# Keys by head in 64x32 tiles, z and W as full products, and the last units of a fused attention and expert kernel ahead of their outputs

## The chip, the cores and the metric

The kernel runs on one core of a Trainium2 chip. The metric is the device time of one execution in microseconds. Its engines are named as in the profile: PE multiplies matrices, PEld loads PE's weights, DVE, ACT and POOL work element by element, SP only issues transfers. The transfers of a queue are issued in the order of its instructions.

## The reference

Two stages follow one another. The first is an attention without softmax: each query and key is multiplied by two small matrices S1 and S2, and the outer product of the two results is its feature vector of 64. The second is a gated feed-forward layer on the heads put side by side.

```python
batch, n_heads, seq, head_dim = (4, 4, 1088, 32)   # r = 8

def phi(x):
    a = np.einsum('rd,bhsd->bhsr', S1, x)
    b = np.einsum('rd,bhsd->bhsr', S2, x)
    return np.einsum('bhsi,bhsj->bhsij', a, b).reshape(*x.shape[:-1], r * r)
q_p, k_p = (phi(q), phi(k))
kv = np.einsum('bhsf,bhsd->bhfd', k_p, v)
z = np.sum(k_p, axis=2)
num = np.einsum('bhsf,bhfd->bhsd', q_p, kv)
den = np.einsum('bhsf,bhf->bhs', q_p, z)[..., None] + 1e-06
x = (num / den).transpose(0, 2, 1, 3).reshape(4352, 128)

gate = np.maximum(x @ w_gate, 0.0)                 # 128 -> 1536
val = x @ w_val
out = gate * val @ w_out                           # 1536 -> 128, float32
```

## The kernel before, in words

**The attention, one batch at a time.** A batch's keys lie on 128 partitions as two heads by 64 tokens, two pairs of heads beside each other (`load_pairs`), 17 tokens on each partition. DVE transposes them in blocks of 32 (`ke_t1`), PE multiplies them by S1 and S2 (`ke_ab`, L448) in float32, in four tiles of the array of 64 rows by 64 columns (a "64x64 tile"), first for one pair of heads and then for the other, both added up in the same two PSUM banks. DVE transposes the result back to tokens on partitions (`ke_t2`, L460, tile `abk`). POOL (for batch 0 partly DVE, from a copy in PSUM) forms the outer products `kp` (L329), PE multiplies them with v (`ke_kv`, L552), DVE masks the result into `kv_bd`. For the denominator PE multiplies `abk` with a part of itself (`ke_z`, L507: nine float32 products in 128x64 tiles, the even ones on one column tile and the odd ones on the other), DVE masks it (`zd`, L519), PE multiplies it by S1 (`ke_w`, L524: two products in 128x64 tiles), and DVE writes that as a further column of the weights `wst` with which the queries are multiplied (`ke_wst`, L532). So numerator and denominator of the queries of a batch wait for its z and W.

The queries come in groups: batch 0 in four pieces (1, 1, 2 and 4 token columns), batches 1 to 3 in one group each, and a last group with the remaining ninth column of all four batches. For each group DVE transposes q (`qt`), PE multiplies by `wst` (L653, the last group L658), DVE transposes back (`abq`, L668), DVE or POOL form `bw`, `dn`, `rd`, `an` and the outer products `qp`, these are transposed (by PE and ACT for batch 0 and the last group, L712 and L753; by a transfer on SP for the others, L742) into `pt`, PE multiplies with `kv_bd` (L719, L725: "num"), and ACT writes `xT` (L761).

**The feed-forward, in 102 units.** A unit is one bank of 512 values: one to four gate products (g) and as many value products (L791), a relu on ACT into `g_sb` (L802), a product on DVE into `ht` (L811), and four output products (L822, "out") that add into bank 7 (`OB`). After the 6 to 24 units of a part ACT evicts the bank (`e_evict`, L839) and SP stores it; the last group's store is four transfers, two on SP and two on ACT (L850), one for each batch.

**What sets the order.** All this is written down as tasks with estimated durations, a due time and a number of banks, and a small planner (`Plan`) puts them in an order by start times that it reckons itself; each engine then runs its instructions strictly in that order. Units are due every 830 ns from 12.5 us on; attention tasks become due backwards from the units that need them. The eight banks are shared: the attention may hold 3 once units run (`a_max`), units hold at most 5 (`f_max`), and 7 of the 8 are given out. In the gaps before the first unit PE runs products of zeros (L871) to keep its clock up.

**Loads.** k and q of batch 0 are loaded first by SP, v of batch 0 by POOL with a cast to float16 on the way (L261, L262), then POOL issues six loads of gate and value weights and later one of the output weights. The other batches' k, q and v are loaded by SP behind a small transfer that waits for the first weights; their v is cast by ACT (L546), each batch with its own buffer. ACT and, for batch 0, DVE zero the padding of some tiles (`fills`).

Of the kernel before, what the change touches and what calls it, by code (L numbers as in the profile page):

```python
# [9 lines left out]
FP32 = mybir.dt.float32  # L10
# [28 lines left out]
class Plan:  # L39
# [46 lines left out]
    def run(self, first_f):  # L86
# [13 lines left out]
        def find(t, now):  # L100

            held = sum(1 for o in owner if o == t.kind)
            most = self.f_max if t.kind == "f" else self.a_max if started_f else self.n_banks
# [26 lines left out]
        total = len(self.tasks)  # L130
        while len(out) < total:
# [48 lines left out]
            if t.kind == "f":  # L180
                started_f = True
            clock[t.eng] = est + t.occ
# [11 lines left out]
def kernel(  # L194
# [20 lines left out]
    T = 64  # L215
    C = S // T
    CA = (C + 1) // 2
    CB = C - CA
    NG = 10
    NH = 14  # L220
    Q0 = 4
# [15 lines left out]
    k_sb = [const.tile([128, 2, C * D], FP32, name=f"k_sb{b}") for b in range(B)]  # L237
    q_sb = [const.tile([128, 2, (C + 1) * D], FP32, name=f"q_sb{b}") for b in range(B)]
    v_sb = [const.tile([128, H, CA * D], FP16, name=f"v_sb{b}") for b in range(B)]
    v32 = [const.tile([128, H, CA * D], FP32, name=f"v32_{b}") if b else None for b in range(B)]  # L240
# [4 lines left out]
    def load_pairs(eng, dst, src, b, hp=None):  # L245
        x = src[b].rearrange("(x y) (t c) d -> (y t) x (c d)", y=2, c=C)
        if hp is None:
            eng.dma_start(out=dst[:, :, 0:C * D], in_=x)
        else:
            eng.dma_start(out=dst[:, hp, 0:C * D], in_=x[:, hp])  # L250
# [8 lines left out]
    def load_v(eng, dst, b):  # L259
        x = v[b].rearrange("h (t c) d -> t h (c d)", c=C)  # L260
        eng.dma_start(out=dst[0:T], in_=x[:, :, 0:CA * D])  # L261
        eng.dma_start(out=dst[T:128, :, 0:CB * D], in_=x[:, :, CA * D:])  # L262
# [3 lines left out]
    load_pairs(nc.sync, k_sb[0], k, 0, 0)  # L266
    load_pairs(nc.sync, k_sb[0], k, 0, 1)
    load_q0(nc.sync, 0)
    load_q0(nc.sync, 1)
# [4 lines left out]
    nc.scalar.activation(out=scr, in_=zero[0:1, 0:1], func=ACTF.Relu)  # L274

# [4 lines left out]
    maskz = const.tile([128, H, R], FP32, name="maskz")  # L280
    mz2 = const.tile([128, 2, H, R], FP32, name="mz2")
    nc.gpsimd.memset(mz2, 1.0)
    nc.gpsimd.affine_select(out=mz2, in_=mz2, compare_op=ALU.is_ge, fill=0.0, base=0,
                            pattern=[[-64, 2], [-2 * R, H], [0, R]], channel_multiplier=1)
    nc.gpsimd.affine_select(out=mz2, in_=mz2, compare_op=ALU.is_ge, fill=0.0, base=R - 1,
                            pattern=[[64, 2], [2 * R, H], [0, R]], channel_multiplier=-1)
# [6 lines left out]
    sk = const.tile([128, 2 * 5 * 2 * R], FP32, name="sk")  # L293
    s1r = const.tile([128, 2, D], FP32, name="s1r")
    wst = [const.tile([128, 2, 2, 32], FP32, name=f"wst{b}") for b in range(B)]
    kt = [const.tile([128, 2, C + 1, 32], FP32, name=f"kt{b}") for b in range(B)]
    abk = [const.tile([128, CA, 2, 32], FP32, name=f"abk{b}") for b in range(B)]
    kp = [const.tile([128, 2, CA, 128], FP16, name=f"kp{b}") for b in range(B)]
    zd = [const.tile([128, H * R], FP32, name=f"zd{b}") for b in range(B)]
# [3 lines left out]
    nc.vector.memset(sk, 0.0)  # L303
# [8 lines left out]
    nc.vector.tensor_tensor(out=maskz, in0=mz2[:, 0], in1=mz2[:, 1], op=ALU.add)  # L312

    def fills(b):
        for x in (wst[b], (v32[b] if b else v_sb[b])[T:128, :, CB * D:], kt[b][:, :, C], kv_bd[b]):
            if b == 0:
                nc.vector.memset(x, 0.0)
            else:
                shape = list(x.shape)
                z = zero[128 - shape[0]:128, 0:1]  # L320
                for _ in shape[2:]:
                    z = z.unsqueeze(1)
                nc.scalar.copy(out=x, in_=z.to_broadcast(shape))
# [22 lines left out]
    def pool(n):  # L346
# [3 lines left out]
    land = dict(k00=4100.0, k01=4800.0, q0=6600.0, q0b=8700.0, v0=8900.0, w0=10100.0, w1=11600.0,  # L350
                w2=13500.0, k1=15800.0, wo=17500.0, q1=21000.0, v1=24500.0, k2=25500.0, q2=27000.0)
# [5 lines left out]
    def e_s1(t):  # L357
        nc.tensor.matmul(ps[:, t.bank, 0:2 * D], sel.rearrange("r x f -> r (x f)"),
                         s16[:, 0:2].rearrange("f p d -> f (p d)"), start=True, stop=True)
# [3 lines left out]
    t_s1c = P.add("s1c", "ACT", **act(64), deps=[t_s1], frees=[t_s1],  # L363
                  emit=lambda t: nc.scalar.copy(out=s1r.rearrange("p a d -> p (a d)"),
                                                in_=ps[:, t_s1.bank, 0:2 * D]))
# [5 lines left out]
    def e_sk(t):  # L371
        for a in range(2):
            masked(sk.rearrange("p (x y) -> p x y", x=2)[:, :, 32 * a:32 * a + 2 * R], a)
# [9 lines left out]
    def prep(b):  # L383
        f = P.add(f"fill{b}", "ACT", 1100, 1170, emit=lambda t: fills(b), after=[t_w0[0]])
# [9 lines left out]
    l_v0 = P.add("ld_v0", "POOL", 1350, 1350, emit=lambda t: load_v(nc.gpsimd, v_sb[0], 0))  # L394
    prev = l_v0
# [6 lines left out]
    l_v0.due = 2000.0  # L402
# [7 lines left out]
    def e_later(t):  # L410
        nc.sync.dma_start(out=gate[:, 0, 0:8], in_=wg[0:1, 0:1, 0:16].bitcast(FP32))
        load_pairs(nc.sync, k_sb[1], k, 1)
        nc.sync.dma_start(out=gate[:, 1], in_=k_sb[1][0:1, 0:1, 0:16])
        load_pairs(nc.sync, q_sb[1], q, 1)
        load_v(nc.sync, v32[1], 1)
        load_pairs(nc.sync, k_sb[2], k, 2)
        load_pairs(nc.sync, q_sb[2], q, 2)
# [3 lines left out]
    for n, e in (("v2", lambda t: load_v(nc.sync, v32[2], 2)),  # L421
                 ("k3", lambda t: load_pairs(nc.sync, k_sb[3], k, 3)),
# [483 lines left out]
```

## Time and profile before

| what | us |
|---|---|
| median of 3 runs (lowest, highest) | 108.33 (108.26, 111.96) |
| the profiled execution, its own time | 108.27 |
| its span, first to last instruction | 106.6 |
| first gate product on PE | 13.03 |
| last gate or value product on PE starts | 99.70 |
| last output product starts | 101.26 |
| last eviction by ACT | 101.69 to 102.07 |
| 102 products of DVE for the units, mean of one | 0.673 |
| 102 relus of ACT, mean of one | 0.605 |

Spans of the profile are in microseconds, means of one instruction often in nanoseconds. A busy PE does not mean that it is at its peak. A group of instructions is named by its line, engine and operation, with out<-in by the program's names. "x18" counts instructions: a float32 product is two on PE, one for each pass over the columns. In the timeline and the chain of waits the first number is the start and the second the length of a merged stretch; in brackets stands how long the engine had been idle before and what ended that.

### The profile page before, as it was taken

To read this page: it belongs to the slowest core of one execution; us is meant where nothing else is said; L and a number is where in the kernel's file an instruction comes from. 1 tells how busy PE (TensorE), PEld (TensorE's weight loads), DVE (VectorE), ACT (ScalarE), POOL (GpSimd) and SP (SyncE) were. 2 spreads that over 40 slices of the span, in tenths; PEclk is the share of its full clock that TensorE was granted. 3 is DMA by queue.
4 is the path that set the end of the run, shared out by engine and by line. 5 is a ranking of instruction groups with operands and counts; after the bars stand their busy time and mean duration, and the time that the engine had idled before them with its cause. 6 is when DMAs were issued, how large, how long until landed. Compare 5 with 4: busy or idle time off the path is not lost.

```text
span 106.6 us, 3081 instructions
## 1 busy us (share of the span) xinstructions
PE 98.5 (92%) x1166; PEld 65.9 (62%) x1166; DVE 91.6 (86%) x199; ACT 78.8 (74%) x158; POOL 47.1 (44%) x69
## 2 busy tenths in 40 slices
PE   6998999999999999999999999999699999999810
PEld 6767788776565655655566656667365666569500
DVE  4669979999998998999999999999668988988900
ACT  4468289569982875999948859997689869899510
POOL 6999260899396950129729402296000004000000
PEclk9999999999999999999999999999999999999985
DMA  1999998992015899910580040004812100400400
GB/s 31 303 207 198 225 220 230 242 360 71 3 49 106 97 222 341 337 40 3 132 163 6 0 102 0 0 0 102 168 32 58 43 6 0 98 0 6 98 26 26
DMA packets 15999, 11.60 MB, mean 109 GB/s; under 512 B 8816, under 2 KB 13296, under 8 KB 15984
## 3 DMA queue, kind: packets, MB, share of 16 engines
q1 hardware_dynamic: 12824, 9.87, 36.7%
q0 software_dynamic: 2960, 1.46, 10.3%
q8 instruction: 9, 0.15, 0.6%
q10 hardware_dynamic: 200, 0.07, 0.3%
q14 instruction: 6, 0.05, 0.1%
HBM read 9.05 MB, written 2.23 MB: 106 GB/s over the span
## 4 chain that ended last, share of the span: by engine, by line
PE 72%; DVE 7%; DMA 7%; POOL 4%; issue 4%; DVEq 1%; SPq 0%; ACT 0%; POOLq 0%
PE ps L791 37%; PE ps L822 18%; PE ps L448 5%; DMA pt<-qp 4%; PE ps L653 3%; PE ps L719 3%; DMA k_sb<-in_k_dram 3%; POOL qp L329 3%; PE ps L507 2%; DVE abq L668 1%; PE ps L712 1%; DVE kp L329 1%; PE ps L552 1%; DVEq L901 1%; DVE qp L329 1%
## 5 line engine op out<-in xcount | busy, mean ns | idle before, releaser
L811 DVE TENSOR_TENSOR ht<-g_sb,ps 128x512 f16<-128x512 f16 x102 | 64.7, 673 | 4.9 <-ACT g_sb L802 2.2
L802 ACT ACTIVATE g_sb<-ps 128x512 f16<-128x512 f32 x102 | 58.6, 605 | 12.0 <-PE ps L791 10.1
L822 PEld LDWEIGHTS <-ht 128*128 128x128 f16 x408 | 29.7, 98 | 19.0 <-DVE ht L811 3.2
L822 PE MATMUL ps<-wo,ht 128*128 128x128 f16 x408 | 38.7, 219 | 0.4 <-DVE ht L811 0.4
L791 PE MATMUL ps<-xT,wv 128*128 128x512 f16 (+2 forms) x132 | 37.2, 331 | 0.0
L791 PE MATMUL ps<-xT,wg 128*128 128x512 f16 (+2 forms) x132 | 36.5, 331 | 0.0
L329 POOL TENSOR_TENSOR kp<-abk 128x640 f16<-128x640 f32 (+1 forms) x14 | 16.3, 1200 | 3.5 <-DVE abk L460 3.5
L329 POOL TENSOR_TENSOR qp<-an,abq 128x512 f16<-128x512 f32 x16 | 16.7, 1070 | 0.5
L678 POOL TENSOR_TENSOR bw<-abq 128x128 f32<-128x128 f32 (+1 forms) x9 | 3.8, 421 | 27.6 <-DVE abq L668 26.8
L791 PEld LDWEIGHTS <-wv 128*128 128x128 f16 x132 | 11.6, 98 | 3.2 <-issue 1.4
L791 PEld LDWEIGHTS <-wg 128*128 128x128 f16 x132 | 11.7, 98 | 1.9
L871 PE MATMUL ps<-zero 128*128 128x128 f16 x75 | 7.0, 254 | 1.1 <-DVE zero L272 1.1
L695 POOL TENSOR_TENSOR an<-abq,rd 128x256 f32<-128x256 f32 (+2 forms) x6 | 2.9, 480 | 11.2 <-DVE rd L692 11.2
L839 ACT ACTIVATE o_sb<-ps 128x512 f32<-128x512 f32 (+2 forms) x11 | 5.6, 505 | 2.4 <-PE ps L822 2.1
L668 DVE STREAM_TRANSPOSE abq<-ps 128x512 f32<-128x512 f32 (+2 forms) x11 | 6.4, 588 | 0.8 <-PE ps L653 0.7
L761 ACT CAST xT<-ps 128x512 f16<-128x512 f32 (+2 forms) x11 | 5.4, 493 | 2.1 <-PE ps L719 2.0
L438 DVE STREAM_TRANSPOSE kt<-k_sb 128x544 f32<-128x544 f32 x8 | 5.7, 731 | 0.9 <-DMA k_sb<-in_k_dram 0.9
L871 PEld LDWEIGHTS <-zero 128*128 128x128 f16 x75 | 5.6, 116 | 1.2 <-DVE zero L272 1.1
L719 PE MATMUL ps<-pt,kv_bd 128*128 128x512 f16 (+2 forms) x20 | 5.1, 337 | 1.1 <-DMA pt<-qp 1.1
L448 PE MATMUL ps<-kt,sk 64*64 64x288 f32 x64 | 5.4, 424 | 0.3 <-DVE kt L438 0.3
L753 ACT COPY pt<-ps 128x256 f16<-128x256 f16 (+2 forms) x5 | 2.9, 583 | 3.1 <-DVE abq L668 1.7
L653 PE MATMUL ps<-qt,wst 64*64 64x256 f32 (+3 forms) x112 | 4.9, 302 | 0.0
(75 smaller groups left out, 68.4 us busy)
## 6 DMA issues: line engine op xcount, KB each, us to landing
out_dram<-o_sb SPq DMA_DIRECT2D x14, 128.0 KB, 2.4
k_sb<-in_k_dram SPq DMA_DIRECT2D x3, 544.0 KB, 5.4
q_sb<-in_q_dram SPq DMA_DIRECT2D x3, 544.0 KB, 5.8
v<-in_v_dram SPq DMA_DIRECT2D x3, 288.0 KB, 5.0
v<-in_v_dram SPq DMA_DIRECT2D x3, 256.0 KB, 5.2
k_sb<-in_k_dram SPq DMA_DIRECT2D x2, 272.0 KB, 3.0
q_sb<-in_q_dram SPq DMA_DIRECT2D x3, 128.0 KB, 3.0
wg<-in_moe_w_gate_dram POOLq DMA_DIRECT2D x3, 128.0 KB, 5.3
```

Of the source, the lines that this page charges most:

```text
L329: eng.tensor_tensor(out=dst.rearrange("s x (i j) -> s x i j", i=R), in0=a[:, :, :, None].to_broadcast([128, n, R, R]), in1=b[:, :, None, : ...
L438: nc.vector.transpose(kt[b][:, hp, 0:C].rearrange("p c t -> p (c t)"), k_sb[b][:, hp])
L448: nc.tensor.matmul(ps[64 * st:64 * st + 64, first.bank + h2, 0:CA * 32], sk[r, 64 * hp:64 * hp + 64], kt[b][r, hp, CA * st:CA * st + CA].r ...
L653: nc.tensor.matmul(o, wst[G.bs[0]][r, hp].rearrange("p a f -> p (a f)"), G.qt[r, hp, st], start=True, stop=True, skip_group_check=True)
L668: nc.vector.transpose(G.ab[:, lo:hi].rearrange("p x h f -> p h x f"), ps[:, f.bank:f.bank + 2, lo * 32:hi * 32].rearrange("p h (x t) -> p ...
L719: nc.tensor.matmul(o, kv_bd[G.bs[0]][:, 2 * hp:2 * hp + 2].rearrange("f a d -> f (a d)"), G.ptc[:, hp, c0:c0 + n], start=hp == 0, stop=hp ...
L791: nc.tensor.matmul(ps[:, t.bank, y * W:(y + 1) * W], w[:, j], xT[:, p.col:p.col + W], start=True, stop=True)
L802: nc.scalar.activation(out=U.g_sb, in_=ps[:, g.bank], func=ACTF.Relu)
L811: nc.vector.tensor_tensor(out=U.ht, in0=U.g_sb, in1=ps[:, vv.bank], op=ALU.mult)
L822: nc.tensor.matmul(ps[:, OB, s * DM:(s + 1) * DM], U.ht[:, y * n * 128 + s * 128:y * n * 128 + (s + 1) * 128], wo[:, j], start=(j == 0 and ...
L839: nc.scalar.mul(out=o_sb[:, 0:n], in_=ps[:, OB, 0:n * DM].rearrange("p (s m) -> p s m", s=n), mul=1.0 / (XSCALE * XSCALE))
L871: nc.tensor.matmul(ps[:, OB, 0:128], zero, zero, start=True, stop=True)
```

## The change

Keys and their values lie differently: 128 partitions are four heads by 32 tokens (34 tokens on each), so that one transfer brings whole rows. The projection of keys uses 64x32 tiles: eight tiles (two pairs of heads by four groups of tokens), each with 9 x 32 columns, written once instead of added up over two. z takes two chunks of `abk` at a time as one full 128x128 product with 64 columns (five instead of nine, the tenth chunk is zeros), W two full products added up, and `wst` is written in two DVE instructions for the two halves of the partitions. Batch 0's v is loaded in float32 by four transfers, two on SP between the two parts of q and two on ACT, and cast by ACT; v of later batches comes by four transfers instead of two, and batches share two buffers. The k feature products are cut along tokens instead of head pairs. In the planner units hold up to 7 banks once no attention task is left, and gate, value, relu and product of unit u above 90 are due (u - 90) x 400 ns earlier, their outs not. The last group has an output bank of its own, is evicted in two halves by ACT and DVE and stored by two transfers of two batches each. Landing times and durations in the planner are changed too.

```diff
-            most = self.f_max if t.kind == "f" else self.a_max if started_f else self.n_banks
+            most = (self.f_max if n_att else self.n_banks) if t.kind == "f" else self.a_max if started_f else self.n_banks
...
-    load_pairs(nc.sync, k_sb[0], k, 0, 0)
-    load_pairs(nc.sync, k_sb[0], k, 0, 1)
+    load_k(nc.sync, 0, 0)
+    load_k(nc.sync, 0, 1)
     load_q0(nc.sync, 0)
+    load_v(nc.sync, 0, 0, 2)
     load_q0(nc.sync, 1)
...
     nc.scalar.activation(out=scr, in_=zero[0:1, 0:1], func=ACTF.Relu)
+    load_v(nc.scalar, 0, 2, 4)
...
-    l_v0 = P.add("ld_v0", "POOL", 1350, 1350, emit=lambda t: load_v(nc.gpsimd, v_sb[0], 0))
...
+    def load_v(eng, b, lo=0, hi=4):
+        x = v[b].rearrange("h (t c) d -> t h (c d)", c=KC)
+        for g in range(lo, hi):
+            n = min(CA, KC - CA * g) * D
+            eng.dma_start(out=v32[b % 2][32 * g:32 * g + 32, :, 0:n],
+                          in_=x[:, :, CA * g * D:CA * g * D + n])
...
+        def ke_ab(t, b, lo, hi, first):
+            for g in range(lo, hi):
+                for hp in range(2):
+                    r = slice(64 * hp, 64 * hp + 64)
                     nc.tensor.matmul(
-                        ps[64 * st:64 * st + 64, first.bank + h2, 0:CA * 32],
-                        sk[r, 64 * hp:64 * hp + 64],
-                        kt[b][r, hp, CA * st:CA * st + CA].rearrange("p c t -> p (c t)"),
-                        start=hp == 0, stop=hp == 1, skip_group_check=True)
+                        ps[32 * g:32 * g + 32, first.bank + hp, 0:CA * 32],
+                        sk[r].rearrange("p h f -> p (h f)"),
+                        kt[b][r, CA * g:CA * g + CA].rearrange("p c t -> p (c t)"),
+                        start=True, stop=True, skip_group_check=True)
...
         def ke_z(t, b, lo, hi, m):
-            for c in range(lo, hi):
-                x = c % 2
-                ab = abk[b][:, c].rearrange("p h f -> p (h f)")
-                nc.tensor.matmul(ps[64 * x:64 * x + 64, m.bank, 0:H * R], ab,
-                                 ab.rearrange("p (h f) -> p h f", h=H)[:, :, R:2 * R],
-                                 start=c < 2, stop=c >= CA - 2, skip_group_check=True)
+            for y in range(lo, hi):
+                nc.tensor.matmul(ps[:, m.bank, 0:2 * H * R],
+                                 abk[b][:, 2 * y:2 * y + 2].rearrange("p c x f -> p (c x f)"),
+                                 abk[b].rearrange("p c x (h f) -> p (c x h) f", h=2)[
+                                     :, 8 * y:8 * y + 8, R:2 * R],
+                                 start=y == 0, stop=y == CA // 2, skip_group_check=True)
...
         def ke_w(t, b, z):
+            for x in range(2):
+                nc.tensor.matmul(ps[:, z.bank, 64:64 + H * R],
+                                 s1r.rearrange("p a d -> p (a d)"),
+                                 zd[b][:, x * H * R:(x + 1) * H * R],
+                                 start=x == 0, stop=x == 1, skip_group_check=True)
...
         def ke_wst(t, b, z):
             for h2 in range(2):
+                r = slice(64 * h2, 64 * h2 + 64)
+                nc.vector.tensor_tensor(
+                    out=wst[b][r, :, :, 2 * R:3 * R],
...
+            ahead = max(0, u - AHEAD) * 400.0
+            g.due, vv.due = due - ahead, due - ahead + 220
...
-            o = P.add(f"out{u}", "PE", 230, 230 + 170, kind="f",
-                      deps=[mult, last_evict if i == 0 else None, ],
+            o = P.add(f"out{u}", "PE", 230, 230 + 170, kind="f", banks=1 if final and not own else 0,
+                      deps=[mult, last_evict if i == 0 and not final else None],
...
+        def e_last(t, G, x):
+            o_sb = f_o.tile([128, 4, DM], FP32, name="o_sb")
+            src = ps[:, own[0].bank, x * DM:(x + 1) * DM]
+            if x == 0:
+                nc.scalar.mul(out=o_sb[:, 0], in_=src, mul=1.0 / (XSCALE * XSCALE))
             else:
+                nc.vector.tensor_single_scalar(o_sb[:, 0], src, 1.0 / (XSCALE * XSCALE), op=ALU.mult)
+            dst = out[2 * x * S:2 * (x + 1) * S].rearrange("(t c) m -> t c m", c=C)
+            (nc.sync, nc.scalar)[x].dma_start(out=dst[:, G.c0], in_=o_sb[:, 0])
```

## The prediction

> **What bounds the kernel now.** I read the busy shares first, then the stretches, then the chain of waits in order of time, and last the timeline of the start and of the end.
>
> ```profile
> PE 98.5 (92%) x1166; PEld 65.9 (62%) x1166; DVE 91.6 (86%) x199; ACT 78.8 (74%) x158; POOL 47.1 (44%) x69
> ```
>
> PE is the busiest engine, DVE is not far behind. Stretches (from:to, length, then busy time of PE, PEld, DVE, ACT, POOL, the granted clock, DMA share, GB/s):
>
> ```profile
> 20.00:40.00 20.00, 20.00 (x239) 12.99 (x238) 19.33 (x39) 14.78 (x27) 16.27 (x17) 1.00 0.58 138
> ...
> 76.00:77.10 1.10, 0.04 (x2) 0.02 (x2) 0.50 (x1) 0.44 (x1) 0.00 (x0) 1.00 0.97 183
> 77.10:90.00 12.90, 12.90 (x138) 7.98 (x139) 10.86 (x19) 10.77 (x20) 0.83 (x3) 1.00 0.15 32
> 90.00:102.00 12.00, 11.26 (x125) 8.04 (x122) 10.07 (x16) 9.99 (x20) 0.85 (x1) 1.00 0.19 45
> ```
>
> From 13 to 76 us PE has no gap at a clock of 1.00, so each 0.1 us of PE work taken out there is 0.1 us of the end, as long as DVE (idle 0.67 us in 20 to 40) keeps up. PE stands still only at 76 to 77 and after 99.
>
> ```profile
> 36.61 0.70 PE ps L507 x18
> 39.38 0.23 PE ps L524 x4
> 51.78 0.65 PE ps L448 x8
> 53.94 0.65 PE ps L448 x8
> 72.35 4.69 DMA pt<-qp
> ```
>
> These are pieces of the chain of waits (start, length): z (L507), W (L524) and k's projection (L448), batch by batch. Batch 1's projection stands there in one piece of 1.13 us.
>
> ```profile
> 6.27 0.29 PEld L358 LDWEIGHTS ps<-s,sel 16*128 16x128 f32 x2 [0.44 <-issue]
> 6.27 0.43 PE L358 MATMUL ps<-s,sel 16*128 16x64 f32 x2
> 7.07 0.66 PEld L507 LDWEIGHTS ps<-abk 128*64 128x64 f32 x18
> 7.89 0.18 DVE L519 TENSOR_TENSOR zd<-ps,maskz 128x32 f32<-128x32 f32 x1
> 8.59 0.18 DVE L532 TENSOR_TENSOR wst<-ps,maskw 128x32 f32<-128x32 f32 x1
> ...
> 101.26 0.40 PE L822 MATMUL ps<-wo,ht 128*128 128x128 f16 x4 [0.20 <-DVE ht L811]
> 101.69 0.38 ACT L839 ACTIVATE o_sb<-ps 128x256 f32<-128x256 f32 x1 [1.52 <-PE ps L822]
> 102.11 1.11 SPq L850 DMA_DIRECT2D out_dram<-o_sb  x2
> 102.11 1.39 ACTq L850 DMA_DIRECT2D out_dram<-o_sb  x2
> ```
>
> The timeline (start, length) shows what one full 128-column float32 weight load costs: two loads of 182 ns each (mean of L358's group) end after 0.29 us, so the second began 0.11 after the first. The 18 loads of 64 columns (137 ns) go in pairs on two column tiles: nine pairs in 0.66, some 0.06 a pair.
>
> The sum is made on the profiled execution: span 106.6, time 108.27, 1.67 around the span; the median of the runs is 108.33.
>
> **k's projection in 64x32 tiles (L448).** A float32 product is two passes. Now eight records (four tiles, two passes) take 0.65, so sixteen take 1.13 in one piece and 1.30 in two. With eight tiles at a time sixteen records are again two rounds: some 0.70. Batches 1 to 3: (1.13 + 1.30 + 1.30) - 3 x 0.70 = 1.6, and for batches 2 and 3 the second entry into a tile mode goes too; I take **-1.7**. No row shows eight tiles; the nearest is the four, where eight records of 424 ns each (their mean) fit into 0.65, so rounds set the time and not records. If only four run together it is still four rounds in one piece, -0.35. [...]
>
> **z and W as full products (L507, L524).** z was 9 products, 18 records; it becomes 5 full ones, 10 records of 128 columns each. By L358's 0.11 the loads alone are 10 x 0.11 = 1.1, plus 0.05 for the last product, against 0.70: +0.45, less some 0.15 because nothing changes the tile mode before and behind it and the first load can run under the product ahead: +0.3 a batch. By L507's 0.06 it would be 0.65: -0.1 with the modes. By the distance of L358's two products (0.43 less one product of 0.27 = 0.16) it would be 1.65: +0.95. I take 0.11, since it is the only row with 128 float32 columns; W, four records, then goes from 0.23 to 0.44, less the modes: +0.1 (-0.05 to +0.45). Three batches: **+1.2**. Middle together: -1.7 + 1.2 = **-0.5**; ends -2.1 and +2.5.
>
> [...]
>
> **The start (batch 0, on the path).** The second transpose of k, the projection and its transposes stand as before (7.26). The q transposes move ahead of them into DVE's idle 0.84 at 5.57, but q's 0.8 us lay beside z before, so nothing is gained. z: loads from 7.07, ten of 0.11, one product and 0.22 of latency end at 8.4, and zd goes from 7.89 to 8.4: +0.5. From zd to wst are 0.52 now; W's four loads add 0.25, and wst written twice (64 partitions each) some 0.15 on DVE. Ten kv products (37 ns each, with two mode changes) now stand on PE between the q projections of the first two groups, on which DVE's next transpose waits: +0.3; against it kp on POOL starts at 7.0 instead of 7.56, being freed of 1.43 us of v issues, and no longer lies beside bw (0.48, its twin 0.19): -0.3. **+0.9**, from +0.2 (loads at 0.06) to +2.0 (0.16).
>
> **v of batch 0 by SP and ACT, cast on ACT.** ACT issues two loads in its idle 1.34 before sk (0.55 to 0.70 each): 0 to +0.1. Behind them on ACT's queue wait sk and all fills. The casts (2 x 0.7) need v at some 8.0 to 9.2 (issued by SP from 3.1, 5.0 to landing); behind them the fills of batches 2 and 3 (1.2 each) end at about 12.4, and the copy of pt, now at 11.93, would be due at 12.8: hidden by the late start. Without that cover it costs 0.5. On SP the v loads stand ahead of q's second part, needed only at 12.8 (landed 8.4). Weights are issued 1.4 earlier, unused. Later v's go by four issues instead of two (0.6 each) on a queue that waits 54 us for ACT's results; k, q and v behind them land microseconds before use. The two shared v buffers wait for casts long done. All of this: 0. DVE gets 0.15 to 0.2 more a batch (wider zd, double wst); its idle time before 76 hides it, else +0.5.
>
> **The wait at 76.** Batch 3's num waits for the transposed pt; the wait is 1.05 us. The chain runs from its q projection over two DVE transposes, POOL, dn, rd, POOL and the DMA. In the changed order two ht products instead of three stand between those transposes (0.62 less), and 17.5 instead of 18 units of PE work cover it (0.2 less). **-0.4**, 0 to -1.
>
> **The last units.** After the last wv product PE waits for ht: the outs start 0.60 apart (DVE's pace) for 0.22 of work, three such waits, 1.1 us in all. In the changed order gates and values run up to 4.4 us earlier by their due times and eight outs stand last, 8 x 0.22 = 1.8 us of PE work that covers DVE's last products. DVE has idle time in 90 to 102 (1.9 us) to be moved into. **-0.9**; 0 if DVE or ACT (9.99 of 12) sets the pace anyway, -1.1 if all goes. The own bank takes away the wait of the last group's first out for the eviction at 97.60, which PE covered: 0.
>
> **The end.** Two evictions side by side (0.28, the rows for 128x128) replace 0.38: -0.1. Each queue issues one store instead of two (1.39 in all on ACT, of which the first is over after 0.55 to 0.6): **-0.8** with the eviction; -0.3 if a store of 128 partitions takes longer to issue.
>
> Sum: +0.9 - 0.5 - 0.4 - 0.9 - 0.8 = -1.7; 108.27 - 1.7 = **106.6 us**. Ends of its own terms: start +0.5 to +1.3, middle -1.2 to 0, the last three -2.6 to -1.2: 105.0 to 108.4.
>
> **Rivals.** *Cheap full loads:* z and W go at 0.06 a load: +0.2 - 2.1 - 0.4 - 0.9 - 0.8 = -4.0, 104.3. For it speaks that L507's pairs do load 128 columns in 0.06; against it that those are two tiles. *Eight tiles do not run together,* so the change doesn't do what it says: middle +0.85, 108.27 + 0.9 + 0.85 - 2.1 = 107.9. For it: no row shows them; against: four start within one piece now. *Slower:* load and product of a full float32 record don't overlap, 0.16 each, on PE, in every batch: start +2.0, middle +2.5, less 2.1 = +2.4, 110.7. For it speaks the distance of L358's two products; against, that the first of them also has its own start in it. It decides from about 0.158 a record on.
>
> **How the numbers follow.** Forecast 0.50, cheap loads 0.20, no eight tiles 0.12, slower 0.12, something else 0.06. A measurement of this kernel can tell about 2% from no change: 106.2 and 110.5. The forecast's own span has some 0.4 of its weight below 106.2 (0.20), with cheap loads (0.20) and a part of the rest (0.05) faster 0.45; slower 0.12; the rest 0.43. Range 104.2 to 108.6: it leaves out the slower rival and a little at the other side.
>
> **What would show it.** z's ten loads 0.11 apart (1.1 in the chain) and batch 0's zd near 8.4; k's sixteen records in 0.7; the first gate product near 14 instead of 13.03; PE's wait before batch 3's num at 0.6; the last outs 0.22 apart; one store a queue, the end 4 us behind the last eviction. Wrong would be the forecast if DVE's idle time is used up before 76 and PE waits for ht in the middle, or if ACT's fills hold the first copy of pt.

## The result and the profile after

| | before | after |
|---|---|---|
| median (lowest to highest) of 4 runs each, us | 108.97 (108.26 to 111.96) | 114.28 (113.83 to 114.65) |
| ratio, 95% interval | | 1.051 (1.041 to 1.061) |
| profiled execution: time, span | 108.27, 106.58 | 114.65, 112.60 |
| start: span's start to first gate product | 13.08 | 20.84 |
| first gate product to last output product | 88.36 | 87.66 |
| last output product to the end of the span | 5.14 | 4.10 |

(13.08 is the first gate product itself; its weight load begins at 13.03. 101.44, from which the last two rows of before are reckoned, is the last of the four output products that begin at 101.26.)

A ratio compares only the runs within 1.5% of the fastest of their kernel, while medians are of all runs.

The change is 5% slower where 1.5% faster had been forecast, and the table says where: 7.76 us are lost before the first gate product, 0.70 + 1.04 are won behind it, and 0.36 more lie outside the span (2.05 against 1.69; nothing here explains that). 7.76 - 0.70 - 1.04 + 0.36 = 6.38, the difference of the two profiled executions.

First the busy shares of the page of after, and its row of the clock that PE was granted, in 40 slices (9 is 90% or more of the full clock):

```profile
PE 104.5 (93%) x1139; PEld 73.1 (65%) x1139; DVE 92.3 (82%) x203; ACT 78.9 (70%) x161; POOL 46.0 (41%) x67
...
PEclk9999999999999999999999999999999999999999
```

PE is busy for 6 us more than before, with 27 instructions fewer (1166 before). Something makes its instructions longer, and the clock row doesn't show it: the trace holds no record of the clock ahead of 20.16 us here and ahead of 4.38 in before, and the rows read 1.00 where there is none. The stretches of after (from:to, length, busy time of PE, PEld, DVE, ACT, POOL, granted clock, DMA share, GB/s):

```profile
1.00:20.00 19.00, 17.62 (x175) 14.30 (x176) 9.53 (x47) 7.77 (x27) 8.93 (x20) 1.00 1.02 221
20.00:40.00 20.00, 19.93 (x269) 15.25 (x267) 18.21 (x37) 15.90 (x33) 12.83 (x16) 1.00 0.36 88
83.00:85.50 2.50, 0.93 (x8) 0.48 (x7) 1.89 (x4) 0.95 (x2) 0.00 (x0) 1.00 0.95 158
```

In the first stretch DVE works half of the time and the DMA engines all of it (a share of 1.02). The start in the timeline of PE (start, length; in brackets the idle time before and what ended it):

```profile
4.17 0.82 PE L902 MATMUL ps<-zero 128*128 128x128 f16 x6
5.43 2.44 PE L458 MATMUL ps<-kt,sk 64*32 64x288 f32 x16 [0.45 <-DVE kt L446]
...
8.53 0.93 PE L902 MATMUL ps<-zero 128*128 128x128 f16 x7
10.25 2.39 PE L518 MATMUL ps<-abk 128*128 128x64 f32 x10 [0.80 <-DVE abk L475]
...
20.32 0.39 PE L902 MATMUL ps<-zero 128*128 128x128 f16 x4
```

The first of these lines was, in before:

```profile
4.17 0.59 PE L871 MATMUL ps<-zero 128*128 128x128 f16 x6
```

And DVE in after:

```profile
5.92 0.71 DVE L446 STREAM_TRANSPOSE kt<-k_sb 128x512 f32<-128x512 f32 x1 [0.63 <-DMA k_sb<-in_k_dram]
9.29 0.51 DVE L642 STREAM_TRANSPOSE qt<-q_sb 128x128 f32<-128x128 f32 x2 [2.66 <-DMA q_sb<-in_q_dram]
9.72 0.80 DVE L475 STREAM_TRANSPOSE abk<-ps 128x320 f32<-128x320 f32 x2
```

Two things stand out. DVE stands still for 2.66 us for q; its next instruction, the transposes of k's projection, needs no q but stands behind it in DVE's order, and PE's z waits for that. And PE runs at half its pace: the identical products of zeros follow each other every 107 ns until 20.2 us and every 56 ns from then on; before, that turn came at 4.4 (seven of them take 0.93 at 8.53, four 0.39 at 20.32, and before six took 0.51 at 6.64). So z takes 2.39 for what takes 1.06 in the next batch. In the chain of waits of after (start, length):

```profile
2.62 6.57 DMA q_sb<-in_q_dram
...
25.90 0.65 PE ps L458 x16
...
28.42 1.06 PE ps L518 x10
...
30.37 0.42 PE ps L537 x4
...
80.31 5.00 DMA pt<-qp
```

The middle answers the prediction's rows: a batch's whole projection is 0.65 in one piece, z 1.06 to 1.11, W 0.36 to 0.42. The wait for batch 3's `pt` grew instead of shrinking; the timeline there:

```profile
77.04 4.15 POOL L339 TENSOR_TENSOR qp<-an,abq 128x512 f16<-128x512 f32 x4
...
79.10 1.11 SPq L866 DMA_DIRECT2D out_dram<-o_sb  x2
80.31 3.69 SPq L755 DMA_TRANSPOSE pt<-qp  x2
...
85.36 0.59 PE L732 MATMUL ps<-pt,kv_bd 128*128 128x512 f16 x2 [1.57 <-DMA pt<-qp]
```

The first half of `qp` is done at 79.13, but two output stores are just being issued on SP, and the transposing transfers begin behind them at 80.31, 1.18 later. Before, two such stores held them up as well, by 0.67. And the end:

```profile
106.75 1.97 PE L842 MATMUL ps<-wo,ht 128*128 128x128 f16 x32
...
108.75 0.28 ACT L872 ACTIVATE o_sb<-ps 128x128 f32<-128x128 f32 x1 [0.76 <-PE ps L842]
109.06 0.29 DVE L874 TENSOR_SCALAR o_sb<-ps 128x128 f32<-128x128 f32 x1 [0.86 <-ACT o_sb L872]
109.24 0.53 SPq L876 DMA_DIRECT2D out_dram<-o_sb  x1
```

Eight outs run back to back. The two halves of the eviction don't run side by side: DVE's begins 0.31 after ACT's, released by it.

### The profile page after: what moved, and what is told of

Read it like the earlier page. It is cut to its first block, busy times and chain, and to the rows that moved or that the text cites. A ratio compares the mean times of both kernels' runs of the same rounds, so it can differ in the third digit from the quotient of the medians.

```text
span 112.6 us, 3039 instructions
## 1 busy us (share of the span) xinstructions
PE 104.5 (93%) x1139; PEld 73.1 (65%) x1139; DVE 92.3 (82%) x203; ACT 78.9 (70%) x161; POOL 46.0 (41%) x67
## 3 DMA queue, kind: packets, MB, share of 16 engines
q0 software_dynamic: 2416, 1.18, 7.9%
## 4 chain that ended last, share of the span: by engine, by line
PE 72%; DMA 10%; POOL 4%; DVE 4%; issue 3%; ACT 1%; SPq 1%; DVEq 0%; POOLq 0%; ACTq 0%
PE ps L810 32%; PE ps L842 18%; DMA q_sb<-in_q_dram 6%; PE ps L518 5%; PE ps L666 5%; DMA pt<-qp 4%; PE ps L902 4%; POOL qp L339 3%; PE ps L732 3%; PE ps L537 2%; PE ps L458 2%; PE ps L565 2%; DVE ht L831 1%; PE ps L725 1%; DVE kt L446 1%
## 5 line engine op out<-in xcount | busy, mean ns | idle before, releaser
L831 DVE TENSOR_TENSOR ht<-g_sb,ps 128x512 f16<-128x512 f16 x102 | 64.0, 673 | 5.1 <-ACT g_sb L822 4.3
L822 ACT ACTIVATE g_sb<-ps 128x512 f16<-128x512 f32 x102 | 58.2, 604 | 11.7 <-PE ps L810 10.0
L842 PEld LDWEIGHTS <-ht 128*128 128x128 f16 x408 | 29.0, 98 | 17.6 <-DVE ht L831 5.4
L842 PE MATMUL ps<-wo,ht 128*128 128x128 f16 x408 | 37.4, 219 | 0.1
L810 PE MATMUL ps<-xT,wg 128*128 128x512 f16 (+2 forms) x132 | 35.3, 330 | 0.1
L339 POOL TENSOR_TENSOR kp<-abk 128x512 f16<-128x512 f32 (+1 forms) x14 | 16.3, 1194 | 8.2 <-DVE abk L475 8.2
L902 PE MATMUL ps<-zero 128*128 128x128 f16 x80 | 9.7, 306 | 1.1 <-DVE maskkv L316 1.1
L902 PEld LDWEIGHTS <-zero 128*128 128x128 f16 x80 | 8.4, 148 | 1.3 <-DVE maskkv L316 1.1
L446 DVE STREAM_TRANSPOSE kt<-k_sb 128x576 f32<-128x576 f32 (+1 forms) x8 | 5.6, 725 | 2.5 <-DMA k_sb<-in_k_dram 2.5
L518 PE MATMUL ps<-abk 128*128 128x64 f32 x40 | 6.1, 310 | 0.8 <-DVE abk L475 0.8
L518 PEld LDWEIGHTS ps<-abk 128*128 128x128 f32 x40 | 5.9, 226 | 1.4 <-DVE abk L475 1.1
```

The source lines that it names most:

```text
L339: eng.tensor_tensor(out=dst.rearrange("s x (i j) -> s x i j", i=R), in0=a[:, :, :, None].to_broadcast([128, n, R, R]), in1=b[:, :, None, : ...
L446: nc.vector.transpose(kt[b][:, lo:hi].rearrange("p c t -> p (c t)"), k_sb[b][:, lo * D:hi * D])
L518: nc.tensor.matmul(ps[:, m.bank, 0:2 * H * R], abk[b][:, 2 * y:2 * y + 2].rearrange("p c x f -> p (c x f)"), abk[b].rearrange("p c x (h f) ...
L810: nc.tensor.matmul(ps[:, t.bank, y * W:(y + 1) * W], w[:, j], xT[:, p.col:p.col + W], start=True, stop=True)
L822: nc.scalar.activation(out=U.g_sb, in_=ps[:, g.bank], func=ACTF.Relu)
L831: nc.vector.tensor_tensor(out=U.ht, in0=U.g_sb, in1=ps[:, vv.bank], op=ALU.mult)
```

## The experiments

Two theories for the start were set against each other. **Loads:** batch 0's new v loads, and weights that are issued 1.4 us earlier, take their share of the 16 DMA engines from k and q. **Pace:** PE doesn't get to its full pace. A third question is the order of DVE. The table collects the start of each kernel; landings are those of the two parts of k and the two transfers of q's first part (a dash: no record). Full pace is given by the trace's records of the granted clock, which agree with the distance of equal products. All in us.

| kernel | k lands | q lands | PE at full pace | first gate product | ratio to before (95%) |
|---|---|---|---|---|---|
| before | 4.10, 4.80 | 5.20, 5.64 | from 4.4 | 13.08 | |
| after | 4.49, 5.90 | 7.44, 9.20 | from 20.2 | 20.84 | 1.051 (1.041 to 1.061) |
| v by POOL | 4.11, 4.76 | 6.04, 6.64 | from 5.7 | 14.39 | 0.990 (0.985 to 0.995) |
| order only | 4.61, 5.92 | 6.87, 8.97 | from 19.6 | 20.30 | 1.046 (1.043 to 1.049) |
| before with v by SP, ACT | -, 5.07 | 6.56, 7.69 | from 4.3 | 13.76 | 1.004 (0.997 to 1.010) |
| 24 fillings | 4.88, 6.68 | 7.14, 8.61 | from 12.3 | 19.35 | none |
| before, no fillings | 4.06, 4.73 | 5.75, 6.85 | from 19.1 | 15.08 | 1.027 (1.022 to 1.032) |
| dense fillings | 4.56, 5.79 | 7.90, 9.64 | 4.9 to 11.7, from 18.5 | 20.00 | 1.008 (1.004 to 1.012) |
| v behind q | 4.01, 4.67 | -, 7.63 | 4.7 to 14.9, from 18.4 | 19.28 | 1.041 (1.034 to 1.048) |
| weights late | 4.62, 5.75 | 7.22, 8.05 | from 16.2 | 18.46 | 1.050 (1.044 to 1.057) |

**v of batch 0 by POOL again.** In the changed kernel:

```diff
-    load_v(nc.sync, 0, 0, 2)
-    load_v(nc.scalar, 0, 2, 4)
+    l_v0 = P.add("ld_v0", "POOL", 2100, 2100, emit=lambda t: load_v(nc.gpsimd, 0, dst=v_sb[0]))
-        K.v = [P.add(f"v{b}{x}", "ACT", **act(2 * CA * D), at=land.get(f"v{b}", 0.0),
+        K.v = [l_v0] if b == 0 else [P.add(f"v{b}{x}", "ACT", **act(2 * CA * D), at=land.get(f"v{b}", 0.0),
```

> The changed kernel, but batch 0's v is again loaded by POOL with a cast, ahead of the weights; everything else of the change stays. Theory A (the added loads of v on ACT's and SP's queues hold up k and q of batch 0, and all else in the start follows): q's first part lands near 5.7 instead of 9.2, the first gate product comes at 14 to 15 instead of 20.8, time 107 to 108.5. Theory B (the full float32 products keep PE at half its pace, whatever the loads): the zero products stay 107 ns apart until well after 10 us, the first gate product comes no earlier than 17, time 110.5 to 112. Theory C (the order of DVE, q's transposes ahead of those of the projected keys): no difference from A here, since q lands in time.

Measured: 107.2 us (106.80 to 107.89, 7 runs), ratio 0.990. In DVE's timeline the wait for q is 1.23 instead of 2.66:

```profile
6.74 0.50 DVE L645 STREAM_TRANSPOSE qt<-q_sb 128x128 f32<-128x128 f32 x2 [1.23 <-DMA q_sb<-in_q_dram]
7.17 0.80 DVE L478 STREAM_TRANSPOSE abk<-ps 128x320 f32<-128x320 f32 x2
```

So this one part of the change, the weights that it lets go out earlier included, costs some 6% (1.051 / 0.990), and the rest of it is worth 1%. First gate product at 14.39, 87.32 from there to the last output product, 3.82 to the end.

**The order of DVE alone.** The changed kernel, the planner told that q lands later (`q0=6150.0` becomes `q0=8000.0`), so that DVE's transposes of k's projection stand ahead of q's.

> The changed kernel, but the planner is told that q of batch 0 lands at 8.0 instead of 6.15, so that DVE transposes the projected keys before q; the loads stay as changed. Theory A, loads: k's second part still lands near 5.9 and q at 9.2, so zd comes near 9.5 instead of 12.75 but q's projection still has to wait for q until about 10; the first gate product near 16 to 18, time 110 to 111.5. Theory C, order alone: the first gate product near 14, time about 107.5. Theory B, pace of PE: first gate near 18, time 111.5 to 112.

Measured: 113.39 (113.32 to 113.45, 2 runs), 1.046. z starts at 9.16 instead of 10.25, but still takes 2.34, and zero products stay at 107 ns until 19.6. The order is worth 0.5 us of the six by the ratios and 0.9 by the medians, and the two intervals overlap.

**The loads alone, in the kernel before.** v of batch 0 in two loads of 64 partitions, one on ACT, one on SP ahead of q's second part, cast by ACT; the weights are issued earlier:

```diff
     load_q0(nc.sync, 0)
+    load_v(nc.sync, v32[0], 0, (0,))
     load_q0(nc.sync, 1)
...
+    load_v(nc.scalar, v32[0], 0, (1,))
```

> The kernel before with one part of the change alone: batch 0's v by SP (between the two parts of q) and ACT, cast by ACT, and so the weights 1.4 us earlier on POOL. Theory A: q's first part lands near 9 here too, DVE waits for it between 7.2 and 9, the first gate product comes 2 to 6 us later than 13.1, time 110.5 to 114. Theory B: the loads alone do little, time 108 to 109.5.

Measured: 108.92 (107.78 to 109.41, 8 runs), 1.004 (0.997 to 1.010): no change. q lands 1.4 to 2.1 us later, as the loads theory says, and yet the first gate product comes only 0.68 later. There DVE has the transposes of k's projection ahead of q's, and PE reaches its full pace at 4.4. So loads as late as these alone don't make the loss; something has to multiply them. They are two loads instead of four, though, and q lands at 7.69 and not at 9.20: loads as late as in after were not tried in the kernel before.

**More fillings behind k's projection.** The changed kernel with 24 more products of zeros behind the second part of k's projection.

> The changed kernel with 24 more zero products on PE behind batch 0's key projection, where PE waits for DVE; loads and order as changed. Theory B: PE reaches its full pace (zero products 56 ns apart instead of 107) near 9 to 10 us instead of 20.3, z's ten loads then take 1.1 instead of 2.2, and the first gate product comes 2 to 3 us earlier, time 111 to 112.5. Theory A alone, with the pace of no weight: no change, 113.5 to 115.

Measured: 112.27 (111.35 and 113.18), without a ratio. The pace turned at 12.3 instead of 20.2, but the fillings, at 107 ns each, stood ahead of the product that s1 needs (11.26 instead of 7.80), and so they held up what they were to speed up. Inconclusive in its size; the next two ask the same without that fault.

**The kernel before without its fillings.** All products of zeros ahead of the first gate product left out (they add nothing to the output); the loads and all else stay.

> The kernel before with all zero products ahead of the first gate product left out; its loads, their order and every other instruction stay. [...] Theory B (only the late loads hold the start; the pace is a side effect): first gate product at 12.8 to 13.3, time within 0.6% of the kernel before.

Measured: 111.49 (111.05 to 112.01, 4 runs), 1.027. PE's timeline:

```profile
4.98 2.20 PE L448 MATMUL ps<-kt,sk 64*64 64x288 f32 x16 [2.19 <-ACT wst L385]
...
7.80 1.27 PE L507 MATMUL ps<-abk 128*64 128x32 f32 x18
...
10.14 1.56 PE L653 MATMUL ps<-qt,wst 64*64 64x32 f32 x48 [0.29 <-DVE wst L532]
```

With 75 products fewer in the whole span PE needs 2.20, 1.27 and 1.56 where it needed 1.33, 0.77 and 0.93. The pace theory holds in kind, and the rival's 12.8 to 13.3 is out: the first gate product comes at 15.08, and the rest of the loss comes behind it, since eight gate products still take 1.02 there and 0.61 only from 19.27 on. In this kernel the missing pace costs 2.9 us (0.027 of 108.4).

**The changed kernel with its gaps filled.** Its loads stay:

```diff
+        for _ in range({'k0ab0': 4, 'k0ab1': 4, 's1': 4, 'k0z0': 6}.get(t.name, 0)):
+            nc.tensor.matmul(ps[:, OB, 0:128], zero, zero, start=True, stop=True)
         if t.emit:
             t.emit(t)
```

> The changed kernel with 18 more zero products, put into the gaps of TensorE ahead of k's projection (4 and 4), s1 (4) and z (6); the loads stay as they are in it (q at some 7.4/9.2). Theory A: TensorE has no gap of more than some 0.3 us from 1.1 to 9 and turns to its full pace (zero products 56 ns apart) before 10; first gate product at 15.5 to 17.5 instead of 20.8; time 109 to 111. Theory B (late loads): pace turns, but the first gate product stays past 19 and the time past 112.5.

Measured: 109.70 median of ten runs, ratio 1.008 against 1.051: 18 products of zeros win 4.6 us. The profile is of one of the three longest runs (112.64 to 113.90), so it shows how the pace is lost again, not the 109.7. In its stretches:

```profile
5.00:9.00 4.00, 3.50 (x43) 1.85 (x40) 1.08 (x2) 1.75 (x8) 1.32 (x3) 1.00 1.18 239
9.00:13.00 4.00, 2.30 (x19) 2.30 (x19) 2.23 (x7) 1.94 (x6) 2.27 (x2) 0.83 1.19 254
13.00:18.00 5.00, 5.00 (x85) 4.53 (x85) 3.01 (x14) 1.50 (x8) 1.30 (x2) 0.50 0.99 152
```

Full pace from 4.9; then PE stands still from 8.84 to 10.70 (DVE waits for q until 9.74), and from 11.68 to 18.51 the granted clock is 0.50. The mean granted clock tells the same of the runs without a profile: 0.954 to 0.969 in the three longest, 0.992 to 1.000 in the other seven. So what this kernel loses depends on whether the wait for q costs it the pace, and the two causes are one chain: late landing, gap in PE, half pace, everything behind it longer.

**Which load.** First all four v loads of batch 0 on SP behind q's second part, weights still early:

```diff
-    load_v(nc.sync, 0, 0, 2)
     load_q0(nc.sync, 1)
+    load_v(nc.sync, 0)
...
-    load_v(nc.scalar, 0, 2, 4)
```

> The changed kernel with all four v loads of batch 0 on SP behind q's second part, none on ACT; the weights are still issued early by POOL, and v is still cast on ACT. Theory A1 (v's loads, on ACT's queue and ahead of q's second part, delay k and q): k lands at 4.1/4.8 to 5.0 and q's first part at 5.3 to 6.2, DVE does not stand still for q, full pace by 7, first gate product at 14 to 15; v lands at 10.5 to 12, so kv_bd comes 1 to 2 later than in the run with v on POOL; time 106.8 to 108.3. Theory A2 (the weights, issued 1.4 earlier, are what delays q): q's first part still past 7, time above 111.

Measured: 113.31 (4 runs), 1.041. Neither side fits whole. k lands as before (4.01, 4.67) and PE is at full pace from 4.7, so it is v's early loads that held k. All profiles say so: the six with a v load on ACT's queue at 1.5 have k's second part at 5.07 to 6.68, the eight without at 4.67 to 4.85. (What ACT's loads and SP's do apart was not run.) But q lands at 7.63 all the same, with the early weights beside it. And v itself comes too late: of its four loads two have a record, issued at 5.26 and 6.35 and landed at 12.18 and 13.39; PE stood still 1.62 us ahead of z, without losing its pace, and then 1.96 us for ACT's cast, and from 14.95 to 18.36 the granted clock was 0.50.

```profile
8.69 1.33 PE L517 MATMUL ps<-abk 128*128 128x64 f32 x10 [1.62 <-DVE abk L474]
```

Then the weights held back, v left on SP and ACT (a memset of an unused tile on POOL ahead of the first weight issue, which moves from 2.95 to 4.68):

> The changed kernel with POOL held by a memset of some 2 us ahead of the first weight issue, so that the weights are issued at the time they had before or later; v stays on SP and ACT. Theory A1 (v's loads on ACT's queue delay k, and q behind it): k still at 4.4/5.8, q past 6.8, no full pace before 15, time 112.5 to 114.5. Theory A2 (the early weights delay q): k as in the changed kernel, q's first part lands before 6.8, DVE's wait for it shrinks by over a microsecond, time 110 to 112.5. Both: between.

Measured: 113.97, 1.050. k at 4.62 and 5.75, q at 7.22 and 8.05: with v's loads in place, later weights bring q forward by 1.15 us, and the time shows nothing of it (1.050 against 1.051). The profile is of the shortest of its four runs (113.34, mean clock 1.000); the other three have a mean clock of 0.954.

So v's early loads delay k, and v's loads and early weights together push q's second transfer to 8.6 to 9.6 (four kernels). What each does to q alone stays open: it lands at 7.63 and 8.05 in these two runs, but also at 7.01 to 7.57 in the four profiles below, which have v by POOL and late weights like the run with 6.64.

**z and W on column tiles again.** On top of v by POOL: nine products of 64 columns for z, two for W, one write of `wst`, in the new layout of k.

```diff
-            for y in range(lo, hi):
-                nc.tensor.matmul(ps[:, m.bank, 0:2 * H * R],
...
+            for c in range(lo, hi):
+                x = c % 2
+                ab = abk[b][:, c].rearrange("p x f -> p (x f)")
+                nc.tensor.matmul(ps[64 * x:64 * x + 64, m.bank, 0:H * R], ab,
...
```

> The run with v on POOL (107.2), and z and W back as products on two column tiles (9 products of 64 columns for z, two for W of 64, one write of wst), in the new layout of k; the 64x32 projection and the rest of the change stay. If full products cost what the trace shows (z 1.06 against 0.70, W 0.42 against 0.23, in each of three batches, and the double write of wst): less 0.55 a batch before the tile modes, which give some 0.1 to 0.2 back, so 1.1 to 1.5 less in the middle and 0.3 to 0.5 at the start: 105.3 to 106.0. Rival (the middle is bound by VectorE by now, and TensorE's work only fills its time): 106.8 to 107.4, with TensorE's idle time before batch 3's num up by a microsecond.

Measured: 106.68 (105.12 to 108.22, 6 runs), 0.977 (0.971 to 0.984), against 0.990: 1.4 us less, at the edge of the 1.4 to 2.0 that were expected; the median itself lies above the range of 105.3 to 106.0. From the first gate product to the last output product it is 85.77 against 87.32. The profile, of the longest run (108.22), lost the pace from 9.00 to 15.83 behind a gap of 1.36 ahead of z:

```profile
8.62 0.99 PE L525 MATMUL ps<-abk 128*64 128x32 f32 x18 [1.36 <-DVE abk L480]
```

This kernel, the next and the last one are the fastest tried (0.977 to 0.983), faster than before and after.

**And DVE's order on top of it** (`q0=7600.0`), to close that gap:

> The run with z and W on column tiles (106.68), with the planner told that q lands at 7.6 instead of 6.15, so that DVE's transposes of the k projection stand ahead of q's. In the profile of that run TensorE stood still for 1.36 us ahead of z while DVE waited for q, and went back to half its pace from 9.6 to 15.9. Theory A (pace): z starts at 7.2 instead of 8.6, TensorE has no gap over 0.7 us up to the first gate product, zero products stay 56 ns apart, the granted clock shows no 0.50, the first gate product comes at 13.4 to 14.2 instead of 16.64 and the time is 104.3 to 105.8 with less spread between its runs (106.68 had 105.1 to 108.2). Rival: q's landing sets the start whatever the order, first gate product past 15, time 106.2 to 107.

Measured: 106.51 (105.79 to 107.31, 6 runs), 0.982 (0.976 to 0.987): not faster than the run before it. The gap and the half pace are gone, and the start is the old one to some hundredths up to `abq` (9.39 in both), but the first gate product comes at 14.69. The expectation missed a new wait, in DVE's timeline and PE's:

```profile
9.74 2.00 DVE L694 TENSOR_TENSOR bw<-abq 128x32 f32<-128x32 f32 x1
```

```profile
11.74 0.70 PE L568 MATMUL ps<-v_sb,kp 128*128 128x64 f16 x18 [1.07 <-POOL kp L342]
```

POOL issues four v loads in 2.35 us where it issued two in 1.43, and stands still for 0.57 us more ahead of its last two weight issues, so its products for `kp` run from 9.14 to 11.67 (from 7.56 in before), and a DVE product that starts in them takes 2.00 us instead of 0.19 and ends when they end.

**The same with the end undone:** no early due times, no lifted bank limit, the shared bank, one eviction and four stores.

> The run before this in the list with the end undone: no early due times for the last units, no lifted bank limit, the last group's outputs in the shared bank, one eviction by ACT and four stores. If the predicted terms for the last units (-0.9) and the end (-0.8) hold, it is 1.2 to 2.2 us slower than the run it is compared with, with three waits of TensorE ahead of the last output products and 5.1 us from the last output product to the end of the span. Rival (DVE or ACT sets the pace of the end anyway): slower by 0.3 to 0.9, by the stores alone.

Measured: 0.998 (0.994 to 1.003) against 0.982, a ratio of 1.017, some 1.8 us. The last output products stand 0.60 apart again, and it is 5.21 from the last of them to the end of the span, against 3.80; from batch 3's num to the last output product it is 24.11 against 23.17.

**kp ahead of the last weights on POOL,** everything else as in the run with DVE's order:

> The run with column tiles and DVE's order changed (106.51), with the last third of the weights issued by POOL behind its two products for kp of batch 0 instead of ahead of them. There kp began at 9.14 and ended at 11.67, TensorE stood still for 1.07 us for it, and DVE's bw product at 9.74 took 2.00 us instead of some 0.19, ending when POOL's kp ended. If POOL's kp is what holds the start now: kp starts at 7.8, ends by 10.4, the bw product's hold shrinks by over a microsecond, first gate product at 13.2 to 13.9 instead of 14.69, time 104.8 to 105.9. Rival (something behind it, the third q group or the copies of pt, holds the first gate as well): first gate 14.3 or later, time 106.2 to 106.8.

Measured: 107.05 (106.27 to 108.05, 6 runs), 0.983 (0.978 to 0.987), no gain. In its profile, of the longest run (108.05), the first gate product comes at 13.47, as expected, but PE then waits for the output weights, which are issued at nearly the same time (11.08 against 11.62) and land at 19.46 against 17.94; why they take longer there is open:

```profile
19.50 0.61 PE L849 MATMUL ps<-wo,ht 128*128 128x128 f16 x8 [2.08 <-DMA wo<-in_moe_w_out_dram]
```

In that run the next limit of the start is thus a landing too.

## Why the prediction was wrong

**The step that failed** is "v of batch 0 by SP and ACT, cast on ACT ... All of this: 0", with the sentence that carried the start, "The second transpose of k, the projection and its transposes stand as before (7.26) ... so nothing is gained". It counted the new loads as issue time on ACT and SP and took every other landing over from the profile of before. In these runs landings moved with what was in flight: ACT's two v loads go out at 1.5 to 3.0, while k is being moved, and not in the idle time from 2.9 on in which the prediction had them, and weights "issued 1.4 earlier, unused" are moved while q is. The second part of k landed 1.10 later, q's first part 3.56. The DMA share of the kernel before from 5 to 10 us, 1.23 (the last but one number), stood in its profile and said that nothing is free there:

```profile
5.00:10.00 5.00, 4.93 (x107) 3.48 (x107) 4.11 (x12) 4.06 (x18) 5.00 (x7) 1.00 1.23 205
```

With v on POOL the start costs +1.31, against +0.9 predicted; the other 6.45 us, put at 0, come with this step.

**What multiplied it** was not in the prediction at all: PE's pace. Before, its first products of zeros run 107 ns apart from 1.06 to 4.4 and 56 ns from there on, without a gap of more than 0.1 in between; after, the turn comes at 20.2. Up to 4.98 PE has the same work without a gap in both, so the late k is not why it didn't turn at 4.4 in after: among the profiles that start with that same work nine have the turn early, anywhere from 4.3 to 5.7. What the late k adds is the gap ahead of its projection. In those nine PE stands still for at most 0.17 us ahead of the turn; in the four kernels with k late and no filling in that gap (after, order only, 24 fillings, weights late) it stands still for 0.45 to 0.84, and the turn doesn't come before 12.3.

That the pace carries the loss is shown from both sides: taking away the fillings costs the kernel before 2.9 us with its loads unchanged, and 18 more give the changed one back 4.6 with its loads unchanged. What sets the turn no run here shows: in after the trace has PE busy without a gap for the ten us from 10.25 to 20.2 (14 with the order alone, from 5.56), and yet at half pace. What loses the pace again they show in part: with column tiles a gap of 1.36 us was enough, while 1.62 with v behind q was not. In the three runs that lost it, 3.41, 6.83 or 10.24 us lie between one change of the clock and the next, whole multiples of 3.41.

**The terms, as run with v on POOL unless said.**

- *k's projection, -1.7:* right; sixteen records in 0.65, so eight tiles run together, and three batches take 1.95 in the chain instead of 3.73.
- *z and W, +1.2:* somewhat more; z takes 3.23 instead of 2.10 in three batches and W 1.14 instead of 0.69, +1.6, as the allowance for tile modes, an estimate of 0.15 a batch, didn't show. Undoing them wins 1.4. The rival of cheap loads (0.06) and that of 0.16 each are both out, as is that of eight tiles not running together.
- *Middle together, -0.5:* not won. From the first gate product to the wait at 76 it is 62.95 in before and in after, and 63.28 with v on POOL; the two terms leave -0.2 of it, and why the feed-forward took up the rest stays open.
- *The wait at 76, -0.4:* wrong in after, where 1.05 became 1.57; with v on POOL it is 0.89. The stores on SP, which the step left out, are one part: they delay the transposing transfers by 1.18 instead of 0.67 us. But they do the same with v on POOL, where the transfers then need 4.37 us to the product instead of 5.05, and why is open.
- *Last units, -0.9:* right; from batch 3's num to the last output product 24.36 became 23.14, and undoing them costs 0.94 there.
- *The end, -0.8:* right in kind, too small; 1.04 in after and 1.32 with v on POOL, though the two evictions ran one after the other.
- *From first gate to last output product* the prediction gives -0.5 - 0.4 - 0.9 = -1.8; after has -0.70, which is 0.0 for the middle, +0.52 for the wait and -1.22 for the last units.

**What would have made it wrong,** by its own list, did not: ACT's fills did not hold the first copy of `pt` (ACT stood idle for 5.58 us ahead of it), and DVE kept some idle time in the middle (busy 19.62 us of 20 from 40 to 60). The forecast, 106.6, is within 0.6 us of the kernel with that one step taken out, and partly by luck: there the start is 0.4 worse than its terms, the stretch to the last output product 0.8 worse and the end 0.5 better. The range, to 108.6, had no room for the step, because the step was booked at 0, with 0.5 for ACT's casts without their cover and nothing for other landings.

## What to carry to other kernels

Where the DMA engines were full (a share of 1.23 from 5 to 10 us in before), loads that were moved to another queue or issued earlier were not free here (q's first part 3.56 us later), and should be priced: find out what is in flight while it is, and whose landing stands first in an engine's order. At the start of this kernel gaps of 0.45 to 0.84 us in PE ahead of its full pace went with a turn at 12.3 us or later, against 4.3 to 5.7 with gaps of at most 0.17; compare the distance of equal products early and late before trusting a duration. Try the parts of an edit one by one: here one costs 6%, one 1.3%, and the rest holds the gain.

## What the runs showed of the hardware

- The clock row said 1.00 in after while equal products were 107 ns apart instead of 56, up to 20.2 us: the trace has no record of the clock until it first turns. It showed 0.50 only behind a stretch at full pace (11.7 to 18.5 us in the run with dense fillings). At this kernel's start that row couldn't be relied on.
- In the three runs that lost the pace again the granted clock changed at whole steps of 3.41 us, counted from its first turn (4.85, 11.68, 18.51 in the run with dense fillings; 4.71, 14.95, 18.36 with v behind q; 5.59, 9.00, 15.83 with column tiles). The length of a gap alone didn't tell here whether the pace was lost: gaps of 1.36 (column tiles), 1.86 (dense fillings) and 1.96 us (v behind q), each within one step, lost it for 3.41 or 6.83 us, while gaps of 1.50, 1.62 and 2.08 us did not (the run with the end undone, v behind q, the last run); the 1.62 us, from 7.07 to 8.69, lay across two steps.
- Full float32 weight loads of 128 columns followed each other every 0.11 us at full pace (0.109 to 0.112 in z of batches 1 and 2 of after) and every 0.213 at half (its batch 0).
- A DVE product of 0.19 us took 2.00 beside two float16 outer products on POOL (9.74 to 11.74 us, POOL's to 11.67, in the run with DVE's order on column tiles), and 0.44 beside the end of them in the last run.
